# Column sums of V's weights moved from the start of a fused attention and mixer kernel into its first head-sum visit

## Chip, cores and metric

The kernel runs on one core of a Trainium2 chip, in one launch. The metric is the device time in microseconds (us), the median of several runs. A core has TensorE (PE, matmul), VectorE (DVE), ScalarE (ACT), GpSimd (POOL) and SyncE (SP), which run side by side and meet at semaphores. Each engine works through its own instructions in order. Transfers are issued by SP, ACT and POOL and carried out by 16 shared DMA engines.

## What is computed

The reference adds three terms over 2048 positions of 512 numbers: the input, a windowed attention with 32 heads of 16 numbers (window of 8 positions, every second one), and a gated mixer. Cut to what matters:

```
xn  = layernorm(x)
qkv = xn @ wqkv                       # q, k, v: 32 heads of 16
logits[s, w] = q[s] . k[s - 2w] / 4   # w = 0..7, masked where s - 2w < 0
o   = softmax(logits) weighted sum of v[s - 2w]
A   = o @ wo
z   = gelu(xn' @ w_in)                # xn' = layernorm(xn)
z1, z2 = z[:, :896], layernorm(z[:, 896:])
B   = (z1 * (w_sp @ z2 + b_sp)) @ w_out
out = x + A + B
```

For the first blocks of 128 rows V is made from the raw input, before the layernorm is known: V = rstd * (x @ wv) - rstd * mean * (column sums of wv). The column sums are the subject of the change.

## The kernel before

**Planner.** The kernel doesn't write its instructions in order. It records tasks (`T` and `dma`, line 503 on), each with an engine, what it reads and writes, an estimated duration and a priority, and `Plan.schedule` (line 123) runs a list scheduling over them. It picks, for each engine, the task that can start first; among tasks that could start within `tol` of it, the one of lowest priority number. Transfers get an assumed landing time, by bandwidth or from a table `land`, written by hand. The result is a fixed order for each engine, and semaphores where a task depends on another. An order that the planner must keep is written out by hand in lists of names (lines 1031 to 1041). The planner's times don't exist at run time; only the orders do. So a change of an estimate, a priority or a landing time moves instructions in places that the diff doesn't show.

**Tiling.** Rows are in 16 blocks of 128 (`b`), or four groups of 512 (`j`). PSUM has eight banks, given to tasks by the planner.

**Start (0 to 18 us).** SP and ACT load x, V's weights in two halves (`wv`, `ldwv0`, `ldwv1`, L532), and the second half of the mixer's weights in two (`ldwin2a`, `ldwin2b`, L538, L544). Seven matmuls on ones (`warm`, L574) run first. For blocks 0 to 2 (`NRAW`), TensorE transposes raw x (`xTx`, L593, four 128x128 matmuls), ScalarE copies the result to SBUF (`xTc`, L620), and `V0` to `V2` (L681, two tasks of two matmuls 128x512 each) multiply by wv. VectorE computes mean and variance (L613, L615), GpSimd `rstd` (L626, a power), VectorE the layernorm (`norm`, L638). From block 1 on the normalized block is transposed by a DMA (`xTd`, L632); from block 3 on V uses it directly. `z2_b` (L793) is the mixer's second half, four matmuls 128x448 for each of two halves.

**Column sums before.** `cs_0` and `cs_1` (L653) are four matmuls of a 128x128 matrix of ones with wv, 512 columns each, in two tasks: `cs_0` behind `xTx0`, `cs_1` between the two halves of `z2_0`. All 128 rows of the result are equal to the column sums. ScalarE writes them, negated, to `ncs` (`cse`, L657). ScalarE writes V's raw products, scaled by rstd, to `vraw` (L688), and VectorE makes `fix0` to `fix2` (L690): V = ncs * (mean * rstd) + vraw. Both inputs are f32 and are read through `hd`, which turns the columns from head by head to the order (number in head, head), a step of 16 elements. GpSimd's queue writes V to DRAM (`Vw`, L695, tensor `vscr`).

**Middle (18 to 97 us).** `Q` and `K` (L704), `z1` (L839) and the other V and z2 blocks fill TensorE. VectorE makes the products of q and k for 8 window positions (`prod`, L725) and adds them over 4 chunks (`padd`, L730), each instruction 128x4096. The sum over heads is TensorE's `red0` (groups 0 and 1) and `red2` (groups 2 and 3) in `logits`, L740: 16 matmuls with a 128x32 matrix `E32`, four side by side on four 32-column strips. The softmax follows (`smax`, `ssub`, L755, L757; `sexp`; `sz`, `srec`, `sattn`, L769 to L779), then a transpose (`attnT`, L781). z2's second layernorm is `z2_wave` (L812 to L825), with a power on GpSimd (`zr`, L822) and `zn` on VectorE (L825).

**Rest (97 to 234 us).** `g` (L935) is the big matmul of the mixer with w_sp, 448 matmuls 128x512; VectorE takes its results (L946, L949) and, in turn, the weighted sums of V (`pv`, L963 to L969), whose inputs `ldVs` (L958) read `vscr` from DRAM. The results are transposed by DMA (`OTd`, L972) and enter the output matmuls (`outo`, `out`, L991, L1000), four and seven for each block; VectorE adds x (`fin`, L1006), and SP stores (L1011).

Of the kernel before, what the change touches and what calls it, by code (L numbers as in the profile page):

```python
# [346 lines left out]
def build_kernel(nc, A_x, A_wqkv, A_wo, B_x, B_w_in, B_w_sp, B_b_sp, B_w_out, out, report=False, emit=True):  # L347
# [17 lines left out]
    vscr = nc.dram_tensor("vscr", (16 + S, 512), BF).ap()  # L365

# [24 lines left out]
    off["ncs"] = off["xcT"] + 512 * NRAW  # L391
    off["vraw"] = off["ncs"] + 1024
# [5 lines left out]
    for name, n in (("prime", 4), ("mx", 128), ("Zb", 256), ("Z", 128), ("maskt", 128), ("st6", NB * 6),  # L398
                    ("mv", NB * 2), ("vpe", NB), ("rstd", NB), ("s1", NB), ("s2", NB), ("m2", NB), ("msq", NB), ("mr", 4),
                    ("vpe2", NB), ("rstd2", NB), ("mhalf", 4)):  # L400
        foff[name] = fb
        fb += n
# [5 lines left out]
    with ExitStack() as es:  # L408
# [74 lines left out]
        for b in range(NRAW):  # L483
            R1(("vraw", b), "vraw", 1024, 1024 * b)
# [87 lines left out]
        for wi in range(NWARM):  # L572
# [14 lines left out]
        def pe_tr(src, keys, name):  # L587
            bk = plan.bank(name)

            def tr(t):  # L590
                last = None
                for dc in range(4):
# [3 lines left out]
            T("pe", tr, reads=keys + ["ident"], writes=[bk], est=4 * c_mm(128), name=name)  # L596
# [10 lines left out]
        def ln_block(b):  # L607
# [9 lines left out]
            if b < NRAW:  # L617
                bc = pe_tr(xin, xk, "xTx%d" % b)
                for h0, hn in ((0, 1), (1, 1)) if b < 2 else ((0, 2),):
                    T("act", (lambda h0, hn: lambda a: a.activation(A("xcT", 256 * hn, 512 * b + 256 * h0),  # L620
                                                                    P(bc, 256 * hn, 256 * h0), ACTF.Copy))(h0, hn),
# [25 lines left out]
        def colsum():  # L647
            bk = plan.bank("cs")
            for hf in range(2):
                def mm(t, hf=hf):  # L650
                    last = None
                    for dc in (2 * hf, 2 * hf + 1):
                        last = t.matmul(P(bk, 512), ones[:, 0:128], A("wv", 512, 512 * dc), start=(dc == 0),  # L653
                                        stop=(dc == 3))
                    return last
                T("pe", mm, reads=[("wv", hf)], writes=[bk], est=2 * c_mm(512) * (1 if hf else 1.6), name="cs_%d" % hf, prio=2)
            T("act", lambda a: a.activation(ncs, P(bk, 512), ACTF.Copy, scale=-1.0), reads=[bk],  # L657
              writes=["ncs"], est=c_act(512), name="cse", prio=-0.5)

        def vraw(b):  # L660
            return A("vraw", 1024, 1024 * b).bitcast(F32)

        def hd(x):
            return x.rearrange("p (h d) -> p d h", d=16)
# [6 lines left out]

        def v_block(b):
            bk = plan.bank("V%d" % b)
            sl = b % 8
            vn = A("Vn" if sl < 4 else "bbc", 512, 512 * (sl % 4))
# [11 lines left out]
            if b < NRAW:  # L687
                T("act", lambda a: a.activation(vraw(b), P(bk, 512), ACTF.Copy, scale=Fv("rstd", 1, b)),  # L688
                  reads=[bk, ("rstd", b)], writes=[("vraw", b)], est=c_act(512), name="Ve%d" % b, prio=4)
                T("dve", lambda v: v.scalar_tensor_tensor(vdh, hd(ncs), Fv("mr", 1, b), hd(vraw(b)), ALU.mult, ALU.add),  # L690
                  reads=["ncs", "mr", ("vraw", b)], writes=[("Vn", sl)], est=690, name="fix%d" % b, prio=1)
            else:
                T("act", lambda a: a.activation(vdh, PC(bk.col(), [[1, 16], [16, 32]]), ACTF.Copy),  # L693
                  reads=[bk], writes=[("Vn", sl)], est=c_act(512), name="Ve%d" % b, prio=4)
            dma("pool", lambda e: e.dma_start(vscr[16 + 128 * b: 16 + 128 * b + 128, :], vn),  # L695
                128 * 512 * 2, ("vwr", sl), reads=[("Vn", sl)], writes=[("vscr", b)], name="Vw%d" % b, prio=1)

        def qk_pair(j, c):
            bk = plan.bank("QK%d_%d" % (j, c), 2)
            for which in range(2):  # L700
                def mm(t, which=which):
# [8 lines left out]
                  est=4 * c_mm(512), name="%s%d_%d" % ("QK"[which], j, c), prio=10 + 18 * j + c)  # L710
# [6 lines left out]
        def prods(j):  # L717
            acc = (0, 2)[j % 2]
            for c in range(4):
# [7 lines left out]
                if c > 0:  # L727
# [3 lines left out]
                      reads=[("pb", 1)], writes=[("pb", acc)], est=c_tt(4096), name="padd%d_%d" % (j, c), prio=5 + j)  # L731
        def logits(j0):
# [11 lines left out]
            T("pe", mm, reads=[("pb", 0), ("pb", 2), "E32"], writes=bks, est=1050.0, name="red%d" % j0, prio=1)  # L744
# [110 lines left out]
        colsum()  # L855
# [30 lines left out]
        for j0 in range(0, NJ, 2):  # L886
# [4 lines left out]
            for j, bk in enumerate(logits(j0), j0):  # L891
                smax(j, bk)
# [138 lines left out]
        for names in (["warm%d" % wi for wi in range(NWARM)] +  # L1031
                      ["xTx0", "cs_0", "V0_0", "xTx1", "V0_1", "xTx2", "V1_0", "V1_1", "xTr0", "V2_0", "V2_1",
                       "z2_0_0", "z2_0_0b", "cs_1", "z2_0_1", "z2_1_0", "z2_1_1", "z2_2_0", "z2_2_1", "V3_0", "V3_1", "z2_3_0", "z2_3_1", "V4_0", "V4_1", "z2_4_0", "z2_4_1", "Q0_0", "Q0_1", "K0_0", "K0_1"],
                      ("rstd7", "Vw0", "Vw1", "Vw2", "Vw3"),
                      ("bnst0", "bnag0", "vpe0", "bnst1", "bnag1", "vpe1", "norm0", "bnst2", "norm1", "bnag2", "vpe2", "bnst3", "norm2",
                       "bnag3", "vpe3", "norm3", "bnst4", "bnag4", "vpe4", "mr", "norm4", "fix0", "fix1", "fix2", "bnst5"),
                      ["bnst%d" % b for b in range(5, NB)],
                      ("xTc0_0", "xTc0_1", "xTc1_0", "xTc1_1", "xTc2_0", "xTe0_0", "xTe0_2", "Ve1", "Ve0", "Ve2",
                       "z2g0", "cse", "z2g1", "z2s0"), ("ldx4", "xTd1", "xTd2", "xTd3", "xTd4", "ldq", "ldk", "ldx5", "ldx6", "ldx7", "ldwin1", "ldx8"), ("ldx15", "xTd5"),
                      *[("ldwin1", "ldx%d" % b) for b in range(9, NB)], *[("z2_4_1", "%s0_%d" % (n, c)) for n in "QK" for c in range(4)],  # L1040
                      ("V10_1", "Q3_3")):
# [4 lines left out]
        plan.schedule(tol=12.0, dma_bw=300.0, dma_lat=1600.0, overlap=35.0,  # L1046
# [53 lines left out]
```

## Time and profile before

| | us |
|---|---|
| median of 3 runs | 236.48 (236.09 to 236.64) |
| profiled execution, its own time | 235.77 |
| its span, first to last instruction | 234.5 |
| TensorE busy in the span | 230.6 (98%) |
| VectorE busy | 208.9 (89%) |
| ScalarE busy | 95.7 (41%) |
| GpSimd busy | 31.6 (13%) |

By stretches of the span, from the windows of the profile:

| us | TensorE | VectorE | ScalarE | GpSimd | DMA share |
|---|---|---|---|---|---|
| 0 to 17.5 | 16.61 | 10.29 | 12.66 | 3.83 | 0.67 |
| 17.5 to 70 | 52.24 | 48.89 | 43.19 | 19.65 | 0.78 |
| 70 to 97 | 26.89 | 26.83 | 21.46 | 8.16 | 0.47 |
| 97 to 120 | 22.89 | 21.89 | 3.60 | 0 | 0.38 |
| 120 to 194 | 73.52 | 70.62 | 14.20 | 0 | 0.98 |
| 194 to 234.5 | 38.42 | 30.40 | 0.60 | 0 | 0.59 |

A row of a timeline has the start, the duration, the engine, the line of the kernel, the operation, output and input tile, shape and count; in brackets stands the idle time ahead of it and what ended it. Matmuls overlap: one 128x512 matmul has a duration of 0.379 us in the rows, while the starts of two that follow each other are 0.216 apart. `PEld` rows are weight loads, which overlap the matmuls. `SPq` rows are issues on a queue; a DMA lands later. The granted TensorE clock is full over the span.

### The profile page before, as it was taken

Reading aid. Unit: us, or ns where it says so; the run is one execution under the profiler, and the core shown is the slowest. Engines: PE = TensorE matmul, PEld = TensorE weight load, DVE = VectorE, ACT = ScalarE, POOL = GpSimd, SP = SyncE. Lnnn points to the kernel's source line nnn. Section 1 sums busy time; section 2 is a strip of 40 time slices with the busy share of each in tenths; the row PEclk is TensorE's granted clock in tenths of the full one; section 3 lists DMA queues with packets and bytes.
Section 4 is the critical chain, followed back from the end, with each engine's and each line's share of the span. In section 5 each row is a group of like instructions: output and inputs, shape, how many; then the busy total and the mean of one; then the engine's idle time right before and its main releaser. Section 6 shows DMA issues by size and latency. Waiting matters only on the chain.

```text
span 234.5 us, 2976 instructions
## 1 busy us (share of the span) xinstructions
PE 230.6 (98%) x1105; PEld 108.6 (46%) x1126; DVE 208.9 (89%) x271; ACT 95.7 (41%) x143; POOL 31.6 (13%) x56
## 2 busy tenths in 40 slices
PE   8999999999999999999999999999999999999996
PEld 3555455555544444444444444444444444444443
DVE  4755899999999999998999898999998998999932
ACT  4898756988895898411020172011111111000000
POOL 2302981023165430000000000000000000000000
PEclk9999999999999999999999999999999999999999
DMA  6769944999305731342299999989899839953542
GB/s 221 204 190 371 247 78 104 184 239 219 79 25 198 251 113 44 67 128 96 53 358 228 261 228 276 180 183 320 250 246 324 256 66 356 310 144 98 170 116 67
DMA packets 83646, 44.26 MB, mean 189 GB/s; under 512 B 55968, under 2 KB 82992, under 8 KB 83632
## 3 DMA queue, kind: packets, MB, share of 16 engines
q1 hardware_dynamic: 82400, 41.66, 69.4%
q0 software_dynamic: 800, 2.11, 2.6%
q10 hardware_dynamic: 432, 0.30, 0.4%
q8 instruction: 9, 0.15, 0.3%
q14 instruction: 5, 0.04, 0.1%
HBM read 26.35 MB, written 4.21 MB: 130 GB/s over the span
## 4 chain that ended last, share of the span: by engine, by line
PE 98%; issue 1%; DVE 0%
PE ps L935 41%; PE ps L704 12%; PE ps L793 10%; PE ps L839 10%; PE ps L1000 10%; PE ps L681 6%; PE ps L991 6%; PE ps L574 1%; PE ps L740 1%; PE ps L593 0%; PE ps L653 0%; DVE arena L1006 0%
## 5 line engine op out<-in xcount | busy, mean ns | idle before, releaser
L935 PE MATMUL ps<-arena 128*128 128x512 bf16 x439 | 96.4, 379 | 0.6 <-issue 0.2
L935 PEld LDWEIGHTS ps<-arena 128*128 128x128 bf16 x448 | 43.7, 98 | 53.1 <-issue 0.4
L943 ACT ACTIVATE arena<-ps 128x1024 bf16<-128x1024 f32 (+1 forms) x16 | 14.7, 917 | 79.8 <-PE ps L935 79.8
L725 DVE TENSOR_TENSOR arena<-arena 128x4096 bf16<-128x4096 bf16 x16 | 36.5, 2290 | 0.1
L963 DVE TENSOR_TENSOR arena<-arena 128x4096 bf16<-128x4096 bf16 x16 | 36.5, 2284 | 0.0
L966 DVE TENSOR_TENSOR arena<-arena 128x2048 bf16<-128x2048 bf16 (+1 forms) x32 | 30.1, 950 | 0.1
L704 PE MATMUL ps<-arena 128*128 128x512 bf16 x124 | 28.6, 379 | 0.2
L730 DVE TENSOR_TENSOR arena<-arena 128x4096 bf16<-128x4096 bf16 x12 | 27.4, 2285 | 0.1
L1000 PE MATMUL ps<-arena 128*128 128x512 bf16 (+2 forms) x117 | 26.9, 366 | 0.1
L793 PE MATMUL ps<-arena 128*128 128x448 bf16 x128 | 25.7, 352 | 0.0
L839 PE MATMUL ps<-arena 128*128 128x512 bf16 x111 | 24.6, 379 | 0.1
L704 PEld LDWEIGHTS ps<-arena 128*128 128x128 bf16 x128 | 14.4, 114 | 13.2 <-ACT arena L693 0.4
L713 ACT ACTIVATE arena<-ps 128x1024 bf16<-128x1024 f32 x16 | 16.3, 1022 | 7.4 <-PE ps L704 7.4
L1006 DVE TENSOR_TENSOR arena<-ps,arena 128x512 bf16<-128x512 f32 (+2 forms) x17 | 11.2, 658 | 8.5 <-PE ps L1000 8.3
L793 PEld LDWEIGHTS ps<-arena 128*128 128x128 bf16 x128 | 12.5, 98 | 12.1
L1000 PEld LDWEIGHTS ps<-arena 128*128 128x128 bf16 x119 | 11.4, 98 | 12.8
L839 PEld LDWEIGHTS ps<-arena 128*128 128x128 bf16 x112 | 10.9, 98 | 13.2 <-ACT arena L845 0.3
L991 PE MATMUL ps<-arena 128*128 128x512 bf16 (+2 forms) x66 | 16.5, 366 | 0.1
L801 ACT ACTIVATE arena<-ps 128x896 bf16<-128x896 f32 x16 | 14.6, 914 | 3.5 <-PE ps L793 3.4
L681 PE MATMUL ps<-arena 128*128 128x512 bf16 x61 | 15.6, 379 | 0.2
L613 DVE BATCH_NORM_STATS2 fpool<-arena 128x6 f32<-128x512 bf16 x16 | 10.8, 680 | 5.5 <-DMA arena<-in_A_x_dram 5.5
L845 ACT ACTIVATE arena<-ps 128x1024 bf16<-128x1024 f32 (+1 forms) x16 | 13.9, 922 | 3.7 <-PE ps L839 3.6
(62 smaller groups left out, 171.7 us busy)
## 6 DMA issues: line engine op xcount, KB each, us to landing
arena<-vscr SPq DMA_DIRECT2D x16, 1024.0 KB, 6.5
arena<-in_A_x_dram SPq DMA_DIRECT2D x30, 128.0 KB, 3.7
vscr<-arena POOLq DMA_DIRECT2D x16, 128.0 KB, 3.1
out_dram<-arena SPq DMA_DIRECT2D x15, 128.0 KB, 1.9
arena<-in_A_wqkv_dram SPq DMA_DIRECT2D x2, 512.0 KB, 4.6
arena<-in_B_w_in_dram SPq DMA_DIRECT2D x2, 448.0 KB, 4.9
arena<-in_B_w_in_dram SPq DMA_DIRECT2D x1, 896.0 KB, 8.2
arena<-in_B_w_out_dram SPq DMA_DIRECT2D x1, 896.0 KB, 5.1
```

Source lines behind the costliest of these rows:

```text
L681: last = t.matmul(P(bk, 512), A("xcT", 128, 512 * b + 128 * dc) if b < NRAW else xTv(b, dc), A("wv", 512, 512 * dc), start=(dc == 0), stop ...
L704: last = t.matmul(P(bk, 512, 512 * which), AC(off["wqk"] + 2048 * which + 512 * dc + c, [[4, 128]]), AC(off["xnT"] + dc * S + 512 * j, [[1 ...
L713: T("act", lambda a: a.activation(AC(qo, [[ko - qo, 2], [1, 512]]), P(bk, 1024).rearrange("p (t n) -> p t n", t=2), ACTF.Copy, scale=0.5), ...
L725: T("dve", (lambda pbv, qb, kb: lambda v: v.tensor_tensor(pbv, qb, kb, ALU.mult))(pbv, qb, kb), reads=rd, writes=[("pb", s_)], est=c_tt(40 ...
L730: T("dve", (lambda av, bv: lambda v: v.tensor_tensor(av, av, bv, ALU.add))(av, bv), reads=[("pb", 1)], writes=[("pb", acc)], est=c_tt(4096 ...
L793: last = t.matmul(P(bk, 448, 512 * hf), xTv(b, dc), AC(off["w_in2"] + 896 * dc + 448 * hf, [[1, 448]]), start=(dc == 0), stop=(dc == 3))
L839: last = t.matmul(P(bk, 512, 512 * i), AC(off["w_in1"] + 896 * dc + 128 * fc, [[1, 128]]), AC(off["xnT"] + dc * S + 512 * j, [[1, 512]]), ...
L935: last = t.matmul(P(bk, 512, 512 * i), AC(off["z2"] + FH * sh + 128 * fc, [[1, 128]]), AC(off["wT%d" % r_] + sh * 512, [[1, 512]]), start= ...
L963: T("dve", lambda v: v.tensor_tensor(tv, tv, av, ALU.mult), reads=[("attn", b)], writes=[("Vs", sv)], est=c_tt(4096), name="pv%d" % b, pri ...
L966: T("dve", (lambda n: lambda v: v.tensor_tensor(A("Vs", n, 4096 * sv), A("Vs", n, 4096 * sv), A("Vs", n, 4096 * sv + n), ALU.add))(n), wri ...
L991: last = t.matmul(P(bk, cn), AC(off["OT"] + 512 * tb + 128 * cc, [[1, 128]]), AC(off["wo"] + 512 * cc + c0, [[1, cn]]), start=(cc == 0), s ...
L1000: last = t.matmul(P(bk, cn), AC(off["z1T"] + fc * S + 128 * tb, [[1, 128]]), AC(off["w_out"] + 512 * fc + c0, [[1, cn]]), start=False, sto ...
```

## The change

1. The matmuls `cs_0` and `cs_1` are gone from the start. The four column-sum matmuls now stand behind the 16 of `red0`, in the same task. Each uses 32 columns of ones and one quarter of wv's rows (128 of 512), on its own 32-column strip: the four strips hold four partial sums, each repeated on 32 rows. The bank (`csbank`) is taken for them.
2. ScalarE's `cse` writes them, negated and in the order (number in head, head), to `ncs`. Four transfers on GpSimd's queue follow, each waiting for what comes before: `csa` writes rows 0, 32, 64 and 96 (4 x 2 KB) to DRAM (`cpart`); `csb` reads them back with four columns to a partition (128 x 4 runs of 16 bytes); two GpSimd adds (`csu`, `csv`) sum the four parts; `csc` writes 512 sums to DRAM (`cscr`); `csr` reads them to all 128 partitions (256 KB).
3. `fix0` to `fix2` wait for `csr`; they are recorded behind `logits(0)`. `vraw` is now written by ScalarE in the new column order, so that VectorE reads and writes contiguously. `Vw0` to `Vw2` follow `csr` and the fixes. V of blocks 0 to 2 has its own place (`Vn0`), in the region of `z1T`, and so have `ncs` and `vraw`.
4. The first transpose `xTx0` is split into two tasks with a bank each, and an eighth warm-up matmul (128 columns) stands behind them.
5. Planner: priority of Q and K of group j from 10 + 18 j to 10 + 30 j; `tol` from 12 to 58, `dma_bw` from 300 to 285, VectorE's `overlap` from 35 to 60; landing times for the four transfers (77.0, 80.5, 83.2, 85.9 us); the lists of orders follow, with `csa` ahead of `zr2` and `csr` ahead of `zr3` on GpSimd. By these, VectorE's `fix0` stands behind the last `padd` of chunk 2 of group 2 and ahead of `zn12`, and TensorE does z2 of blocks 5 to 7 ahead of Q and K of group 1, and all V ahead of `red0`.

```diff
@@ -388,15 +390,16 @@
-    off["ncs"] = off["xcT"] + 512 * NRAW
-    off["vraw"] = off["ncs"] + 1024
+    off["Vn0"] = off["z1T"] + 1536
+    off["ncs"] = off["z1T"] + 3 * S + 1024
+    off["vraw"] = off["ncs"] + S
...
@@ -569,7 +578,7 @@
-        for wi in range(NWARM):
+        for wi in range(NWARM + 1):
...
@@ -615,10 +624,11 @@
-                bc = pe_tr(xin, xk, "xTx%d" % b)
+                bcs = [pe_tr(xin, xk, "xTx0a", (0, 1)), pe_tr(xin, xk, "xTx0b", (2, 3))] if b == 0 else [pe_tr(xin, xk, "xTx%d" % b)] * 2
...
@@ -644,24 +654,25 @@
-        def colsum():
-            bk = plan.bank("cs")
-            for hf in range(2):
-                def mm(t, hf=hf):
-                    last = None
-                    for dc in (2 * hf, 2 * hf + 1):
-                        last = t.matmul(P(bk, 512), ones[:, 0:128], A("wv", 512, 512 * dc), start=(dc == 0),
-                                        stop=(dc == 3))
-                    return last
-                T("pe", mm, reads=[("wv", hf)], writes=[bk], est=2 * c_mm(512) * (1 if hf else 1.6), name="cs_%d" % hf, prio=2)
-            T("act", lambda a: a.activation(ncs, P(bk, 512), ACTF.Copy, scale=-1.0), reads=[bk],
-              writes=["ncs"], est=c_act(512), name="cse", prio=-0.5)
+        def colsum(bk):
+            T("act", lambda a: a.activation(ncs.rearrange("p (d h) -> p d h", d=16), PC(bk.col(), [[1, 16], [16, 32]]), ACTF.Copy, scale=-1.0), reads=[bk], writes=["csp"], est=c_act(512),
+              name="cse", prio=-0.5)
+            dma("pool", lambda e: e.dma_start(cpart, A("ncs", 1024).bitcast(F32)[0:128:32, :]),
+                8192, "csa", reads=["csp"], writes=["cpart"], name="csa", prio=-5)
+            dma("pool", lambda e: e.dma_start(Fv("csq", 16).rearrange("p (q i) -> p q i", q=4),
+                                              bass.AP(tensor=cpart.tensor, offset=cpart.offset, ap=[[4, 128], [512, 4], [1, 4]])),
+                8192, "csb", reads=["cpart"], writes=["csq"], name="csb", prio=-5)
+            T("pool", lambda g: g.tensor_tensor(Fv("csq", 8), Fv("csq", 8), Fv("csq", 8, 8), ALU.add), writes=["csq"],
+              est=200, name="csu", prio=-5)
+            T("pool", lambda g: g.tensor_tensor(Fv("css", 4), Fv("csq", 4), Fv("csq", 4, 4), ALU.add), reads=["csq"],
+              writes=["css"], est=200, name="csv", prio=-5)
+            dma("pool", lambda e: e.dma_start(bass.AP(tensor=cscr.tensor, offset=cscr.offset, ap=[[4, 128], [1, 4]]), Fv("css", 4)),
+                2048, "csc", reads=["css"], writes=["cscr"], name="csc", prio=-5)
+            dma("pool", lambda e: e.dma_start(ncs, bass.AP(tensor=cscr.tensor, offset=cscr.offset, ap=[[0, 128], [1, 512]])),
+                128 * 2048, "csr", reads=["cscr"], writes=["ncs"], name="csr", prio=-5)
...
@@ -685,15 +703,15 @@
-                T("act", lambda a: a.activation(vraw(b), P(bk, 512), ACTF.Copy, scale=Fv("rstd", 1, b)),
+                T("act", lambda a: a.activation(vraw(b).rearrange("p (d h) -> p d h", d=16), PC(bk.col(), [[1, 16], [16, 32]]), ACTF.Copy,
+                                                   scale=Fv("rstd", 1, b)),
                   reads=[bk, ("rstd", b)], writes=[("vraw", b)], est=c_act(512), name="Ve%d" % b, prio=4)
-                T("dve", lambda v: v.scalar_tensor_tensor(vdh, hd(ncs), Fv("mr", 1, b), hd(vraw(b)), ALU.mult, ALU.add),
-                  reads=["ncs", "mr", ("vraw", b)], writes=[("Vn", sl)], est=690, name="fix%d" % b, prio=1)
+                fixes.append((b, vn, vk))
+                return
...
@@ -707,7 +725,7 @@
-                  est=4 * c_mm(512), name="%s%d_%d" % ("QK"[which], j, c), prio=10 + 18 * j + c)
+                  est=4 * c_mm(512), name="%s%d_%d" % ("QK"[which], j, c), prio=10 + 30 * j + c)
...
@@ -729,6 +747,14 @@
+        def fix_all():
+            for b, vn, vk in fixes:
+                def fix(b=b, vn=vn, vk=vk):
+                    T("dve", lambda v: v.scalar_tensor_tensor(vn, ncs, Fv("mr", 1, b), vraw(b), ALU.mult, ALU.add),
+                      reads=["ncs", "mr", ("vraw", b)], writes=[vk], est=690, name="fix%d" % b, prio=1)
+                fix()
+                v_write(b, vn, vk)
...
@@ -741,7 +767,18 @@
+            if j0 == 0:
+                mm0 = mm
+
+                def mm(t):
+                    mm0(t)
+                    last = None
+                    for q in range(4):
+                        last = t.matmul(ps[32 * q:32 * q + 32, csbank.col():csbank.col() + 512], ones[:, 0:32],
+                                        A("wv", 512, 512 * q), start=True, stop=True)
+                    return last
...
@@ -888,7 +925,11 @@
-            for j, bk in enumerate(logits(j0), j0):
+            lgs = logits(j0)
+            if j0 == 0:
+                colsum(csbank)
+                fix_all()
+            for j, bk in enumerate(lgs, j0):
...
@@ -1029,23 +1070,23 @@
-                      ("V10_1", "Q3_3")):
+                      ("V10_1", "Q3_3"), ("csa", "zr2"), ("csr", "zr3")):
...
-        plan.schedule(tol=12.0, dma_bw=300.0, dma_lat=1600.0, overlap=35.0,
+        plan.schedule(tol=58.0, dma_bw=285.0, dma_lat=1600.0, overlap=60.0,
```

More of the change, by code (lines that the diff above doesn't have):

```diff
@@ L483, in build_kernel @@
         for b in range(NRAW):
-            R1(("vraw", b), "vraw", 1024, 1024 * b)
+            R1(("Vn", "raw", b), "Vn0", 512, S * b)
+        R1("csp", "ncs", 1024)
+        for fc in range(FC):
+            for j in range(NJ):
+                R1(("z1T", fc, j), "z1T", 512, fc * S + 512 * j)
+        for b in range(NRAW):
+            R1(("vraw", b), "vraw", 1024, S * b)
         R1("bbc", "bbc", S)
@@ L591, in tr @@
                 last = None
-                for dc in range(4):
+                for dc in dcs:
                     last = t.matmul(P(bk, 128, 128 * dc), src[:, 128 * dc:128 * dc + 128], ident, start=True,
```

48 lines of the change are left out of this document (27 added, 21 removed).

## The prediction

> **What bounds the kernel now.** I read the chain of waits first (page, part 4), then the same chain in order of time, then the timeline where the change acts.
>
> ```profile
> PE 98%; issue 1%; DVE 0%
> ...
> 4.11 0.58 PE ps L653 x2
> ...
> 8.83 0.43 PE ps L653 x2
> ```
>
> The chain is TensorE from end to end, so a matmul taken out is worth its time only if the next one can really start earlier. The column-sum matmuls (L653) stand in it with 0.58 + 0.43 = 1.01 us. Both lie in the first 10 us, where TensorE follows the loads:
>
> ```profile
> 4.09 0.60 PE L653 MATMUL ps<-arena,const-bfloat16-1.0 128*128 128x512 bf16 x2
> 4.59 0.60 PE L681 MATMUL ps<-arena 128*128 128x512 bf16 x2
> 5.31 0.59 PE L681 MATMUL ps<-arena 128*128 128x512 bf16 x2
> ...
> 8.67 0.59 PE L653 MATMUL ps<-arena,const-bfloat16-1.0 128*128 128x512 bf16 x2
> 9.10 1.11 PE L793 MATMUL ps<-arena 128*128 128x448 bf16 x5
> ```
> ```profile
> 3.27 0.51 SPq L544 DMA_DIRECT2D arena<-in_B_w_in_dram  x1
> ...
> 6.89 5.99 SPq L632 DMA_TRANSPOSE arena<-arena  x4
> ```
>
> The second half of V's weights, issued at 1.3, takes the longer of L532's two landings, 3.9: it is there at 5.2, and V0_1 runs at 5.31. The second half of w_in2 takes 5.3 from 3.27 and is there at 8.57. The first transpose takes 2.6 from 6.89 and is there at 9.54; z2_1_0, which needs it, runs at 9.10 + 4 x 0.19 = 9.86.
>
> VectorE is the near rival (89%), so I looked at what it owes TensorE: the head sums (L740), each behind the last `padd`.
>
> ```profile
> 67.10 2.29 DVE L730 TENSOR_TENSOR arena<-arena 128x4096 bf16<-128x4096 bf16 x1
> 69.99 1.05 PE L740 MATMUL ps<-arena 128*32 128x512 bf16 x16
> ...
> 111.75 0.69 DVE L946 TENSOR_TENSOR arena<-arena 128x1024 bf16<-128x1024 bf16 x1 [1.08 <-ACT arena L943]
> 115.16 2.29 DVE L730 TENSOR_TENSOR arena<-arena 128x4096 bf16<-128x4096 bf16 x1
> 119.22 1.05 PE L740 MATMUL ps<-arena 128*32 128x512 bf16 x16
> ```
>
> red0 runs 0.6 behind its padd (69.39), red2 1.77 behind its own (117.45). VectorE has 1.08 of idle time shortly before the second.
>
> **The change, part by part.**
>
> *Start, TensorE.* cs_0 filled a wait. Without it, and with the two transposes of xTx0a evicted first, V0_0 comes some 0.2 earlier, but V0_1 still needs the weights that land at 5.2 and stays at 5.31: gain 0. The split transposes and the eighth warm-up matmul lie in that hole. cs_1 (0.43) goes too; z2_0_1 may then run at 8.67, with its weights landed at 8.57: 8.70. z2_1_0 would follow at 9.46, but its transpose is there at 9.54; V0_1 ran 0.1 behind its landing, so 9.64 instead of 9.86. Everything behind it is back to back and landed earlier (w_in1: 15.60 + 8.2 = 23.8, wanted at 24.3). Start: -0.22, between -0.30 (no delay behind the landing) and 0 (that transpose 0.2 later, with nothing left to fill the hole).
>
> *red0, TensorE.* Four matmuls 128x512 on 32 columns, as L740 has them: 16 took 119.88 - 119.22 = 0.66 to the start of the last four, so four starts lie in 0.22. They extend a visit that is paid anyway: +0.22. Were they not side by side they would cost 4 x 0.216 = 0.86 (L935's start to start), the upper bound; the lower is 0.22. I take 0.22, the same shape in the same instruction stream.
>
> *Order ahead of red0.* The order of instructions gives the changed red0 20 more V matmuls (4.31), 8 more z2 (1.51) and 24 fewer Q/K (5.18): +0.65, so it stands at 69.99 + 0.65 - 0.22 = 70.4. The rest comes behind it instead; ahead of red2 the sums are equal. VectorE's padds up to there are the same, some 0.5 later by the moved masks and `rstd` on GpSimd: 69.9. No stall; the 0.5 left is the margin.
>
> *fix0 to fix2, VectorE.* Before, they ran in a hole:
>
> ```profile
> 11.67 3.15 DVE L690 SCALAR_TENSOR_TENSOR arena<-arena,fpool 128x512 bf16<-128x512 f32 x3
> ```
> ```profile
> L757 DVE TENSOR_TENSOR arena<-ps,fpool 128x1024 bf16<-128x1024 f32 x4 | 4.9, 1220 | 0.0
> L690 DVE SCALAR_TENSOR_TENSOR arena<-arena,fpool 128x512 bf16<-128x512 f32 x3 | 3.1, 1117 | 0.0
> ```
>
> They free 3.1 us nobody used and now stand between padd2_2 and zn12, in the dense stage. Old form: 1.04 start to start, reading f32 at a 64-byte stride. The new form reads and writes contiguously. Bounds: 0.61 (half of L757's elements, less the overlap of 0.08) and 1.04 (its own row). I take 0.61, since L757 also has two f32 sources and the stride is gone: 3 x 0.61 = 1.8. The 1.08 idle ahead of L946 swallows part: red2's padd ends at 117.45 + 1.8 - 1.08 = 118.2, TensorE arrives at 119.2. Cost 0, 1.0 left. At 1.04 each it would end at 119.5: +0.4.
>
> The Trainium skill (SBUF — State Buffer, the note on cachelines under "Door 1: The DMA port swizzle") says an engine pays for each access that crosses to a new 16-byte line; L690 at 1.117 for 512 elements beside L757 at 1.220 for 1024 agrees. By it the fixes cost 0.6 each, the same sum.
>
> *The four transfers, GpSimd's queue.* cse is one ScalarE row of 0.59 (L693's strided read), done at 72.4. Then, in the queue's order: csa, zr2, csb, csu, csv, csc, csr, zr3, Vw0 to Vw2. No row has these shapes.
>
> ```profile
> vscr<-arena POOLq DMA_DIRECT2D x16, 128.0 KB, 3.1
> ...
> arena<-in_B_b_sp_dram SPq DMA_DIRECT2D x1, 512.0 KB, 4.7
> ...
> vscr<-arena POOLq DMA_DIRECT2D x1, 16.0 KB, 1.9
> ```
> ```profile
> 28.59 1.02 POOL L822 TENSOR_TENSOR fpool<-fpool 128x4 f32<-128x4 f32 x1
> ...
> 67.22 3.06 POOL L822 TENSOR_TENSOR fpool<-fpool 128x4 f32<-128x4 f32 x1 [2.27 <-DVE fpool L819]
> ```
>
> csa 2.1 (L695's median between 70 and 82 us; 1.9 to 4.0): 74.5. zr2 holds the queue to 76.0. csb, 512 runs of 16 bytes: 3.1 (1.9, up to 4.0 plus three more issues of 0.54 = 5.6): 79.1. csu and csv: two adds of 0.55 (L626's 128x1 row) plus 0.5 of waiting, since VectorE then does the short L825 rows: 1.6 (0.3, two memsets of 0.15, up to 5.2: two of 0.55 with the whole 3.06 - 1.02 = 2.04 on each): 80.7. csc 2.1 (1.9 to 4.0): 82.8. csr, 256 KB: 3.4, half way between 2.1 and 4.7: **86.2**, bounds 80.5 and 95.9.
>
> fix0 is reached when VectorE has done five padds/prods (2.2 each, start to start), two smax and two ssub (1.13 to 1.25), four L825 (0.43) and the small rows behind 69.9, 17.7 in all: 87.6. So csr is 1.4 early; with red2's 1.0, it may land until **88.6** before TensorE notices. Queued behind csr: zr3 (zn12 to zn15, wanted by g0_0_3 at 99, ready near 92) and Vw0 to Vw2 (landed near 93; ldVs1 was issued at 102.77): covered. New is ScalarE's wait: `ncs`, `vraw` and `Vn0` lie in z1T, so its L845 tasks for groups 2 and 3 wait until the fixes have read (89.5) and Vw0 to Vw2 have landed. The last of these tasks ran at 92.56, 94.29 and 96.02; two of the three writes are in by 92.5, and a held task stops TensorE only when no bank is left for the next group (two banks each, 1.73 us of matmuls). Covered, but narrowly: it falls with the same late csr.
>
> *Tail.* VectorE ends at most 0.8 later than before in the dense stage; OTd15, issued at 222.62, landed some 2.7 later (the transposes' median), at 225.3, and is wanted at 230.2. Covered.
>
> **Sum.** Against the profiled execution, 235.77 (span 234.5 and 1.27 around it): -0.22 + 0.22 + 0 = 235.8. That execution lies 0.71 below the median of the runs, 236.48, so I state **236.5**. Its own range: -0.3 to +0.4, so 236.2 to 236.9.
>
> **Rivals.**
> *A. csr lands late* (slower). VectorE runs in order, so fix0 holds all of softmax and prod3 behind it; past 88.6 each us is one us at red2, and TensorE has no idle time to win it back. For: four round trips in series in the stage where L695's landings reached 4.0, and zr1, zr2, zr3 took 3.0 for the work that took 1.02 at 28.59. With one full block of 2.04 on each add (+3.0) and 1.5 more on csb, csr comes at 90.7: +2.1, 238.6. Against: 2.4 of margin. The Trainium skill (SBUF — State Buffer, "Who interferes with whom") says a VectorE instruction with two SBUF inputs contends with a GpSimd instruction that reads SBUF; the 3.06 beside 1.02 agrees, and by that rule an add issued under a prod or padd waits it out.
> *B. The start gains all it frees* (faster). If the landings did not hold TensorE, 1.01 - 0.22 = 0.79 would be won: 235.7. For: both sums are in the chain. Against: 5.2 and 9.54 above; it needs transfers that land earlier than in this execution.
> *C. The sum matmuls run one by one*: +0.86 - 0.22 = +0.64, 237.1. Against: L740's starts.
> *D. The change's relief is nil and the fixes keep 1.04*: 236.9, inside the forecast's range.
>
> **How the numbers follow.** This kernel's measurement can tell about 0.2% (0.47 us) from no change. Forecast with D, within that: 0.46. A: 0.34. C or another stall (red0's 0.5 margin used up): 0.05. B: 0.15. So faster 0.15, same 0.46, slower 0.39. The range runs from 235.8 (most of B left outside) to 239.4, A with csr at 91.5; about 0.07 lies above.
>
> **What would show it.** V0_1 near 5.31 and z2_1_0 near 9.6: the start. red0 with 20 matmuls near 70.4, some 0.22 longer: the sum. The fixes at 0.69 each: the stride. csr's landing against fix0's start: if VectorE idles ahead of fix0 on a DMA, A is at work, and red2 shows the same delay less 1.0. I am wrong if red2 waits for VectorE, or if z2_1_0 starts before 9.5.

## The result, and the profile after

| | before | after |
|---|---|---|
| median of 22 runs, us | 236.2 (235.71 to 236.83) | 237.41 (236.08 to 238.53) |
| profiled execution, us | 235.77 | 237.73 |
| its span, us | 234.5 | 236.5 |

The ratio is 1.0048, with a 95% interval of 1.0035 to 1.0062: about half a per cent slower. The two profiled executions differ by 1.96, the medians by 1.21: the first profile lies 0.43 below its median, the second 0.32 above its own.

The page of the changed kernel, part 4, the chain that ended last. Before, it was TensorE at 98%.

```profile
PE 74%; DVE 14%; DMA 8%; issue 2%; POOL 1%; ACT 1%; ACTq 0%
```

Transfers and VectorE have entered it. The same chain in order of time (start, duration, what), from the first transfer of the column sums to the second head sum; short pieces called issue, between one transfer and the next, are left out:

```profile
73.18 3.04 DMA cpart<-arena
76.51 5.02 DMA fpool<-cpart
81.89 2.38 POOL fpool L667
84.55 1.70 DMA cscr<-fpool
86.54 3.86 DMA arena<-cscr
90.42 2.08 DVE arena L753 x3
...
121.16 1.05 PE ps L766 x16
```

csa, csb, the adds, csc and csr stand one behind the other, then the fixes (L753), VectorE's products and sums, and red2 (L766). The timeline of the changed kernel shows what each end of this did to its engine:

```profile
71.58 0.39 PE L777 MATMUL ps<-arena,const-bfloat16-1.0 128*32 128x512 bf16 x4
...
81.89 2.37 POOL L667 TENSOR_TENSOR fpool<-fpool 128x4 f32<-128x4 f32 x1
81.91 2.29 DVE L743 TENSOR_TENSOR arena<-arena 128x4096 bf16<-128x4096 bf16 x1
...
90.42 2.08 DVE L753 SCALAR_TENSOR_TENSOR arena<-arena,fpool 128x512 bf16<-128x512 f32 x3 [2.90 <-DMA arena<-cscr]
...
121.16 1.05 PE L766 MATMUL ps<-arena 128*32 128x512 bf16 x16 [1.42 <-DVE arena L748]
```

VectorE idles 2.90 us ahead of the fixes, for csr. 31 us later TensorE idles 1.42 ahead of red2, for VectorE: an engine that is busy from there on passes its delay to the next meeting point. By the starts of TensorE's matmuls, the 1.96 us divide into +0.07 at the start, +0.22 in red0's visit, a wait of 0.16 ahead of the matmul at 93.67 (z1, whose ScalarE evictions stand behind the fixes), and +1.49 at red2: 1.94 in all.

### The profile page after: what moved, and what is told of

Read it like the earlier page. It is cut to its first block, busy times and chain, and to the rows that moved or that the text cites. A ratio compares the mean times of both kernels' runs of the same rounds, so it can differ in the third digit from the quotient of the medians.

```text
span 236.5 us, 3005 instructions
## 1 busy us (share of the span) xinstructions
PE 232.0 (98%) x1127; PEld 108.3 (46%) x1127; DVE 207.2 (88%) x271; ACT 95.9 (41%) x143; POOL 33.4 (14%) x62
## 4 chain that ended last, share of the span: by engine, by line
PE 74%; DVE 14%; DMA 8%; issue 2%; POOL 1%; ACT 1%; ACTq 0%
PE ps L976 31%; PE ps L1041 10%; PE ps L830 10%; PE ps L722 9%; PE ps L1032 6%; PE ps L699 5%; DVE arena L748 4%; DVE arena L743 4%; PE ps L876 3%; DMA fpool<-cpart 2%; DMA arena<-cscr 2%; DMA cpart<-arena 1%; DMA arena<-arena 1%; DMA arena<-in_A_x_dram 1%; POOL fpool L667 1%
```

## The experiments

Eleven kernels in three sets, each beside runs of the kernel before on the same chip (medians 236.07, 236.22 and 236.31 in the first, second and third set).

| kernel | set | runs | median, us | ratio (95% interval) |
|---|---|---|---|---|
| free_fix | 1 | 12 | 236.17 | 1.0000 (0.9987 to 1.0012) |
| wide_sums | 1 | 4 | 238.17 | 1.0084 (1.0066 to 1.0102) |
| few_runs | 1 | 6 | 237.65 | 1.0071 (1.0043 to 1.0098) |
| quiet_loads | 1 | 11 | 235.93 | 0.9993 (0.9981 to 1.0005) |
| one_more_trip | 2 | 6 | 240.95 | 1.0169 (1.0130 to 1.0208) |
| wide_pinned | 2 | 12 | 236.60 | 1.0012 (0.9999 to 1.0025) |
| no_sums | 2 | 12 | 237.36 | 1.0026 (1.0001 to 1.0050) |
| planner_only | 2 | 12 | 236.85 | 1.0033 (1.0020 to 1.0045) |
| no_sums_warm | 3 | 12 | 236.03 | 0.9990 (0.9978 to 1.0002) |
| quiet_no_warm | 3 | 12 | 236.10 | 0.9991 (0.9978 to 1.0004) |
| early_trip | 3 | 12 | 236.30 | 0.9997 (0.9981 to 1.0013) |

The ratios are of each kernel to the kernel before in its own set. The runs of no_sums fall into two groups 1.0 us apart, so its median stands for neither.

**Is it the wait for csr? free_fix** takes the wait away: csr writes to a place of its own, and the fixes read what cse wrote. All else stays.

```diff
-            dma("pool", lambda e: e.dma_start(ncs, bass.AP(tensor=cscr.tensor, offset=cscr.offset, ap=[[0, 128], [1, 512]])),
+            dma("pool", lambda e: e.dma_start(ncx, bass.AP(tensor=cscr.tensor, offset=cscr.offset, ap=[[0, 128], [1, 448]])),
...
-                      reads=["ncs", "mr", ("vraw", b)], writes=[vk], est=690, name="fix%d" % b, prio=1)
+                      reads=["csp", "mr", ("vraw", b)], writes=[vk], est=690, name="fix%d" % b, prio=1)
```

> The changed kernel with its instructions in the same order on every queue and all four transfers still made, but the last one writes 448 of its 512 columns to a place of its own, and fix0 to fix2 read what cse wrote. It leaves out the true column sums for blocks 0 to 2. Theory (the fixes wait for the sums, and red2 waits for VectorE): the 2.90 us of VectorE idle ahead of the fixes goes, padd3_3 ends near 118.2 instead of 121.1, TensorE reaches red2 near 119.6 and does not wait, so the 1.58 us gap goes and the 0.16 us one behind it: 235.7 us (235.4 to 236.2). Rival (the fixes' load in the dense stage, or the new order of the stage, costs the time): red2 still waits for VectorE and the time stays at 237.0 or more.

Timeline of free_fix:

```profile
87.19 2.07 DVE L756 SCALAR_TENSOR_TENSOR arena<-arena,fpool 128x512 bf16<-128x512 f32 x3
...
119.25 1.05 PE L769 MATMUL ps<-arena 128*32 128x512 bf16 x16
```

No bracket stands behind either row: the fixes follow the row ahead of them at once, and red2 doesn't wait. The time is that of the kernel before. By the trace every engine runs its instructions in the changed kernel's order, and the trip was late here too (csr issued at 85.03, 4.6 to land, so 89.6). The new order of the dense stage and the fixes' 2.07 us in it therefore cost nothing that can be measured; the wait costs it all.

**What makes csr late? few_runs** reads the four partial sums in longer runs, **quiet_loads** keeps SP's loads out of the way.

```diff
-                                              bass.AP(tensor=cpart.tensor, offset=cpart.offset, ap=[[4, 128], [512, 4], [1, 4]])),
+                                              bass.AP(tensor=cpart.tensor, offset=cpart.offset, ap=[[32, 16], [512, 4], [1, 32]])),
```
```diff
+        for n1 in ["ldbbc"] + ["ldwo%d" % c for c in range(4)] + ["ldxr%d" % c for c in range(4)]:
+            byname[n1].deps.add(byname["csr"])
```

> The changed kernel with csb, the adds and csc on 16 partitions: 64 runs of 128 bytes instead of 512 of 16. If csb's 5.02 us come from its many short runs, it falls toward csa's 3.04, csr lands near 88.4 instead of 90.4, VectorE's idle ahead of the fixes falls from 2.90 to 0.9, padd3_3 ends near 119.1 ahead of TensorE at 119.6, and the time is 235.8 us (235.4 to 236.4). If the length comes from the transfers of SyncE that run beside it, csb keeps 4.5 to 5.0, and the time stays at 237.2 to 237.5.

> The changed kernel with ldbbc, ldwo0 to ldwo3 and ldxr0 to ldxr3 held until csr has landed, so that nothing of SyncE's runs beside the trip. If these loads stretch it, csb falls from 5.02 to 3 and csr from 3.86 to 3, csr lands near 87.6 and the time is 235.8 us (235.4 to 236.4). If they do not, csr lands at 90 or later and the time is 237.2 to 237.5, or more where a held load is itself late.

DMA issues of the changed kernel between 72 and 91 us: size, and us from issue to landing.

```profile
arena<-cscr POOLq DMA_DIRECT2D x1, 256.0 KB, 3.9
...
cpart<-arena POOLq DMA_DIRECT2D x1, 8.0 KB, 3.0
fpool<-cpart POOLq DMA_DIRECT2D x1, 8.0 KB, 5.0
cscr<-fpool POOLq DMA_DIRECT2D x1, 2.0 KB, 1.7
```

The same of few_runs (72 to 96 us):

```profile
arena<-cscr POOLq DMA_DIRECT2D x1, 256.0 KB, 4.7
cpart<-arena POOLq DMA_DIRECT2D x1, 8.0 KB, 3.8
fpool<-cpart POOLq DMA_DIRECT2D x1, 8.0 KB, 4.1
cscr<-fpool POOLq DMA_DIRECT2D x1, 2.0 KB, 2.8
```

And of quiet_loads (72 to 90 us):

```profile
arena<-cscr POOLq DMA_DIRECT2D x1, 256.0 KB, 3.8
...
cpart<-arena POOLq DMA_DIRECT2D x1, 8.0 KB, 1.7
fpool<-cpart POOLq DMA_DIRECT2D x1, 8.0 KB, 2.4
cscr<-fpool POOLq DMA_DIRECT2D x1, 2.0 KB, 1.8
```

In few_runs csb is 0.9 shorter, and the three others took 0.7 to 1.1 longer in that execution; csr landed at 90.46 and nothing was won. About 3 was expected for csb if its short runs were the cause. The 4.1 measured is no gain that can be told from scatter: with the short runs as they were and the same loads beside it, csb took 4.0 in free_fix and 4.4 in one_more_trip. So the short runs are not the cause.

With SP's queue silent csa takes 1.7 instead of 3.0 and csb 2.4 instead of 5.0, and csr lands at 85.46 instead of 90.40. Only SP's transfers have changed their places in the trace of quiet_loads; every other queue keeps its order. Of the 4.94, the two transfers give 3.7 from issue to what follows them; 0.9 comes from the adds, of which VectorE held up one in either kernel, for longer in the changed one, and 0.36 from csa's earlier issue. The packets of the two traces show how the loads act on csb, which is 16 packets of 512 bytes. The first starts 1.53 us after the issue in both (at 78.04 and 76.55). The last starts 3.86 after it in the changed kernel and 1.81 in quiet_loads. In the changed kernel SP's packets start in the same time: those of 4 KB (ldbbc) until 78.37, those of 1 KB (ldxr and ldwo) from 78.51 to 82.17. In quiet_loads SP has none there.

csr itself took as long (3.8 beside 3.9). That doesn't make it free of neighbours: it took 4.7 in few_runs, and 6.6 in early_trip, where the DMA engines were busy throughout (DMA share 1.19 from 45.8 to 52.4). The timeline of quiet_loads at red2:

```profile
119.15 1.05 PE L766 MATMUL ps<-arena 128*32 128x512 bf16 x16
```

Red2 follows TensorE's work without a wait. The held loads (0.5 MB of ldbbc, four of 128 KB for ldxr, and ldwo) were not wanted earlier, so holding them cost nothing. Which of them does most of the harm was not tried. The amount of traffic alone does not say it: the kernel before moved 219 GB/s between 70 and 82 us, and its nine writes of V in that time (128 KB each) took 2.1 us at the median; the changed kernel moved 148 GB/s while csb ran.

**Does the end follow csr one for one? one_more_trip** makes csr later by one transfer.

```diff
+            dma("pool", lambda e: e.dma_start(cscr2.rearrange("(a b) -> a b", a=16), cscr.rearrange("(a b) -> a b", a=16)), 2048, "csd", reads=["cscr"], writes=["cscr2"], name="csd", prio=-5)
...
-                128 * 2048, "csr", reads=["cscr"], writes=["ncs"], name="csr", prio=-5)
+                128 * 2048, "csr", reads=["cscr2"], writes=["ncs"], name="csr", prio=-5)
```

> The changed kernel with one transfer more in the chain: the 2 KB of cscr are copied to a second DRAM buffer before csr reads them from there; nothing else moves. Theory (the end follows csr's landing one for one): the added trip takes 2 to 3 us (csc 1.70, csa 3.04), csr lands at 92.4 to 93.4, red2 waits 2 to 3 us longer, and the time is 239.4 to 240.4 us. Rival (fixes' load or order): under 238.2, since nothing on an engine was added.

The chain of one_more_trip, again without the pieces called issue, and a row of its timeline:

```profile
85.14 4.62 DMA cscr<-cscr
90.05 3.38 DMA arena<-cscr
93.46 2.08 DVE arena L755 x3
```
```profile
96.71 1.89 PE L878 MATMUL ps<-arena 128*128 128x512 bf16 x4 [2.83 <-ACT arena L884]
```

csr lands 3.0 later than in the changed kernel (93.44), and the span is 3.1 longer (239.6). The added transfer took 4.6 where 2 to 3 were expected, and the median, 240.95, is above the range given. That the two differences agree does not show the end following csr one for one, since the place of the charge has moved: TensorE waits at 96.71 for ScalarE's z1 evictions (L884), which wait for the fixes to read `ncs` and `vraw`, and red2 no longer waits for VectorE. The cover that the prediction called narrow is gone here. The windows of one_more_trip add a second charge (columns: stretch; its length; busy us and instructions of TensorE, its weight loads, VectorE, ScalarE and GpSimd; the granted clock; DMA share; GB/s):

```profile
96.70:98.00 1.30, 1.29 (x4) 0.47 (x5) 1.30 (x4) 1.30 (x3) 0.00 (x0) 0.50 0.45 180
98.00:100.00 2.00, 2.00 (x7) 0.76 (x6) 2.00 (x2) 1.46 (x3) 0.00 (x0) 0.59 0.00 0
100.00:101.80 1.80, 1.80 (x10) 0.78 (x8) 1.80 (x2) 1.03 (x2) 0.00 (x0) 1.00 0.05 9
```

After an idle time of 2.83 us (3.21 from one start to the next) TensorE got half its clock for some 3 us: its matmuls come 0.43 apart until 99.65, which costs 1.4. So the 3.1 are made of a wait of 3.0 in the place of 1.65, of 1.4 for the clock, and of 0.2 by which TensorE was later ahead of it. The other runs agree: the two with a mean granted clock of 1.0 took 238.63 and 239.10 us, the three with 0.993 took 240.84 to 241.49, the one with 0.986 took 242.23. A long stall can be paid twice; by these clocks it was in four of the six runs. In the changed kernel, where TensorE idled 1.42, the granted clock behind it is 1.00 (121 to 125 us), and all its runs have a mean of 1.0.

**What do the sums cost when they need no trip? wide_sums and wide_pinned** make them whole in red0's visit.

```diff
-                        last = t.matmul(ps[32 * q:32 * q + 32, csbank.col():csbank.col() + 512], ones[:, 0:32],
-                                        A("wv", 512, 512 * q), start=True, stop=True)
+                        last = t.matmul(P(csbank, 512), ones[:, 0:128],
+                                        A("wv", 512, 512 * q), start=(q == 0), stop=(q == 3))
...
-            dma("pool", lambda e: e.dma_start(cpart, A("ncs", 1024).bitcast(F32)[0:128:32, :]),
-                8192, "csa", reads=["csp"], writes=["cpart"], name="csa", prio=-5)
...
```

> The changed kernel with the column sums made whole in red0's visit: four matmuls with 128 columns of ones, accumulated, and cse writes ncs at once; the four transfers and the two adds are gone. Theory (only the trip is late): no VectorE idle ahead of the fixes, red2 does not wait; the four matmuls cost 0.86 instead of 0.22, so 235.7 + 0.65 = 236.4 us (236.0 to 236.8), no slower than before by more than 0.3. Rival (fixes or order cost it): 237.4 or more.

> wide_sums once more (four matmuls with 128 columns of ones, accumulated, no transfers), now with every engine's instructions held in the changed kernel's order, where wide_sums had been planned anew and TensorE waited 1.3 us for a late transpose at its end. Theory (only the trip is late; order and fixes cost nothing): no wait at red2 and none at the end; the visit costs 0.65 more than four matmuls of 32 columns, so free_fix's 236.17 + 0.65 = 236.8 us (236.4 to 237.1). Rival (the new order itself costs): 237.4 or more.

wide_sums missed its range, 238.17 against at most 236.8. Without the transfers the planner had made another order, and its timeline shows the price at the end:

```profile
232.46 0.82 PE L1019 MATMUL ps<-arena 128*128 128x384 bf16 x4 [1.15 <-DMA arena<-arena]
```

TensorE waits for the last transpose of O by 1.3 us, from the starts of its matmuls. With the order held, in wide_pinned, that wait is gone, as is red2's; the four matmuls cost what was expected:

```profile
70.57 1.05 PE L753 MATMUL ps<-arena 128*32 128x512 bf16 x16
71.55 1.04 PE L764 MATMUL ps<-arena,const-bfloat16-1.0 128*128 128x512 bf16 x4
72.43 1.89 PE L709 MATMUL ps<-arena 128*128 128x512 bf16 x8
```

72.43 - 70.57 = 1.86 for the visit, against 71.91 - 70.71 = 1.20 in the changed kernel: 0.66 more (0.65 expected). The time, 236.60, lies in the range given and below the changed kernel's 237.41 of the earlier runs. The chain of transfers saved 0.66 us of TensorE and cost 1.65.

**Does the planner's new order cost something? planner_only** is the kernel before with the change's settings.

```diff
-                  est=4 * c_mm(512), name="%s%d_%d" % ("QK"[which], j, c), prio=10 + 18 * j + c)
+                  est=4 * c_mm(512), name="%s%d_%d" % ("QK"[which], j, c), prio=10 + 30 * j + c)
...
-        plan.schedule(tol=12.0, dma_bw=300.0, dma_lat=1600.0, overlap=35.0,
+        plan.schedule(tol=58.0, dma_bw=285.0, dma_lat=1600.0, overlap=60.0,
```

> The kernel before with only the planner's settings of the change (due times of Q and K 30 instead of 18 apart, tolerance 58, rate 285, overlap 60); the sums stay at the start. If the moved order of the dense stage costs nothing by itself, 235.8 to 236.4 us; if it were the cause, some 237.3.

```profile
4.08 1.04 PE L653 MATMUL ps<-arena,const-bfloat16-1.0 128*128 128x512 bf16 x2
...
69.73 1.05 PE L740 MATMUL ps<-arena 128*32 128x512 bf16 x16 [0.33 <-DVE arena L730]
```

The timeline shows red0 waiting for its padd, 0.40 by the starts of the matmuls. In this execution the start also came 0.42 later, since the matmuls were 0.4 apart until 5.3 us, cs_0 (L653) among them, where the kernel before has 0.23 from 4.1 on. Together that is its 0.8 of span over the kernel before. How many of the twelve runs had the slower start is not known. The median, 236.85, lies between the two values expected. It doesn't explain the change, whose red0 didn't wait and whose order, in free_fix, ran as fast as before.

**What were the sums worth at the start? no_sums** is the kernel before without them; **no_sums_warm** adds one warm-up matmul behind the first transposes; **quiet_no_warm** takes that matmul from quiet_loads.

```diff
...
-                T("pe", mm, reads=[("wv", hf)], writes=[bk], est=2 * c_mm(512) * (1 if hf else 1.6), name="cs_%d" % hf, prio=2)
-            T("act", lambda a: a.activation(ncs, P(bk, 512), ACTF.Copy, scale=-1.0), reads=[bk],
-              writes=["ncs"], est=c_act(512), name="cse", prio=-0.5)
+            T("pool", lambda g: g.memset(ncs, 0.0), writes=["ncs"], est=600, name="ncs0", prio=-9)
...
```

no_sums_warm has this beside it:

```diff
-        for wi in range(NWARM):
+        for wi in range(NWARM + 1):
...
```

> The kernel before without its column sums: cs_0, cs_1 and cse are gone, GpSimd writes zeros to ncs; it leaves out the correction of blocks 0 to 2 by the sums. Forecast of the prediction: cs_0 fills a wait for wv1 and is worth nothing, cs_1's 0.43 is worth 0.2 to 0.4 as the first transpose then limits, so 235.7 to 235.9 us. Rival (both sums stand on the path): 0.8 to 1.0 less than before, 235.1 to 235.3.

> no_sums with one more warm-up matmul (128x128) behind the first transposes, as the changed kernel has it. In no_sums 8 of 12 runs were at 237.3 to 238.0 and 4 at 235.6 to 236.3; in the profiled slow one TensorE idled 0.82 us ahead of V0_0, and its matmuls of 512 columns came every 0.43 us until 9.5 us, where they come every 0.216 in the kernel before. Theory (what keeps TensorE busy ahead of V0_0 keeps its matmuls fast): with the filler all runs lie at 235.5 to 236.2. Rival (something else of the start, such as a late load): the runs stay split, with 237.3 and more among them.

> quiet_loads (235.93 us) without the warm-up matmul that the change added behind the first two transposes. Theory (the filler keeps the matmuls fast): some or most runs come to 237.5 to 238.2, with matmuls of 512 columns every 0.43 us until about 9.5 us. Rival (a filler in a hole is worth nothing, as the prediction had it): all runs at 235.6 to 236.4.

no_sums became slower: work was taken away, and 7 of its 12 runs lie at 237.3 to 238.0, 5 at 235.6 to 236.3 (8 and 4 in the expectation of no_sums_warm is a wrong count). The timeline of its profiled execution (237.83):

```profile
4.85 1.01 PE L671 MATMUL ps<-arena 128*128 128x512 bf16 x2 [0.57 <-ACT arena L620]
...
7.36 1.91 PE L671 MATMUL ps<-arena 128*128 128x512 bf16 x4
```

The same matmuls in no_sums_warm:

```profile
4.01 0.31 PE L574 MATMUL ps<-const-bfloat16-1.0 128*128 128x128 bf16 x1
4.69 0.61 PE L671 MATMUL ps<-arena 128*128 128x512 bf16 x2 [0.37 <-ACT arena L620]
...
7.10 1.03 PE L671 MATMUL ps<-arena 128*128 128x512 bf16 x4
```

Four matmuls take 1.91 in the one and 1.03 in the other: in no_sums they start every 0.43 us until about 9.5, in no_sums_warm every 0.216 from 4.7 on. With the filler all 12 runs lie at 235.7 to 236.5, the split is gone, and the top is 0.3 above the range expected. So work in cs_0's place had a use that a hole doesn't show: with nothing there (0.82 us by the starts, 0.57 in the bracket) the matmuls stay at half speed for 5 us more in that execution. That it helps by keeping TensorE busy ahead of V0_0 was the theory. The Trainium skill ("TensorE: Matmul & The Clock Gate", "What's actually happening") says the array runs at half clock until a window of about 3.4 us was busy, and that this window runs free, so that the moment varies from run to run; the split runs of no_sums agree. quiet_no_warm went against this theory: with a hole of 0.61 by the starts and no filler all of its 12 runs lie at 235.73 to 236.65. Nor is a full place enough: planner_only, with cs_0 in it, was slow until 5.3 in its profiled execution, and early_trip, with the filler, until 7.0. So the filler was needed in no_sums and not in quiet_no_warm; what exactly decides, the length of the hole or where it falls in time, stays open.

The sums' own worth at the start is 0.28 us by the medians of no_sums_warm (236.03 against 236.31), but its interval reaches past 1 (0.9978 to 1.0002), and in the profiled execution Q0 begins only 0.08 earlier than in the kernel before (17.56 against 17.64). So the 0.2 to 0.4 expected for no_sums is not excluded and not shown; its rival of 0.8 to 1.0 is excluded by the interval.

**Could the trip be made early? early_trip** puts the change's four matmuls at the start and the four transfers on GpSimd's idle time from 33 us on.

```diff
+        for hf in range(2):
+            def csmm(t, hf=hf):
+                last = None
+                for q in (2 * hf, 2 * hf + 1):
+                    last = t.matmul(ps[32 * q:32 * q + 32, csbank.col():csbank.col() + 512], ones[:, 0:32],
+                                    A("wv", 512, 512 * q), start=True, stop=True)
+                return last
+            T("pe", csmm, reads=[("wv", hf)], writes=[csbank], est=250.0, name="cs_%d" % hf, prio=2)
+        colsum(csbank)
...
```

> The changed kernel with the four column-sum matmuls at the start, on 32 columns as in the change: two behind the added warm-up matmul, two behind V0_1; cse follows behind z2g1, and the four transfers and two adds stand on GpSimd behind rstd15, in its idle time from 33 to 44 us. All else keeps its order, SyncE's loads too. Theory: csr lands near 46, 41 us ahead of the fixes, red2 does not wait, and red0's visit is 0.22 shorter than in quiet_loads (235.93), of which the start takes back 0.06 to 0.2: 235.7 to 236.0 us. Rival (the start pays for each matmul that stands in it): 236.2 or more.

Timeline of early_trip:

```profile
4.88 1.03 PE L699 MATMUL ps<-arena 128*128 128x512 bf16 x2
...
88.31 2.07 DVE L753 SCALAR_TENSOR_TENSOR arena<-arena,fpool 128x512 bf16<-128x512 f32 x3
```

csr lands at 52.4 (46 was expected), and the fixes don't wait. But the matmuls at the start hold V0_0 until 4.88, and in this execution the matmuls run at half speed until 7.0 (two take 1.03), so that Q0 begins 1.1 later than in the changed kernel. This execution, at 237.02, is the slowest of the twelve, so it doesn't stand for the median. 236.30 is above the theory's range and in the rival's, but the kernel before is 0.24 slower in this set than in the first, from which the range was worked out; with that the theory's range would end at 236.24, and the two can't be told apart. What is shown is that early_trip equals the kernel before (ratio 0.9997). No kernel here beat the kernel before by more than can be measured; quiet_loads, quiet_no_warm and early_trip bring the change back to its time.

## Why the prediction was partly right

The range, 235.8 to 239.4, held the 237.41. It held it because it was drawn to take in rival A: the likeliest case, no change at 236.5 (0.46), fell, and rival A, csr late (0.34), is what happened.

**The sum matmuls** were right: side by side, +0.216 in red0's visit for the 0.22 forecast.

**The fixes** were right where it mattered: 0.75 each and 2.07 for three, 0.67 start to start where 0.61 was taken, far from the 1.04 of the strided form. They cost nothing in free_fix.

**The margin** was right: VectorE was ready for the fixes at 90.42 - 2.90 = 87.52, where 87.6 was forecast. csr could land until 88.6, it landed at 90.40, 1.8 too late, and TensorE paid 0.16 + 1.49 = 1.65. "I am wrong if red2 waits for VectorE" came true as it was put. The rule of one us at red2 for each us past 88.6 held for this landing and not for the next: at 93.44, in one_more_trip, the wait came at z1 and the clock was charged on top.

**The step that failed** is csr's landing, 86.2 forecast against 90.40. Terms of that sum, forecast and measured: cse done 72.4 and 72.9; csb's issue 76.0 and 76.51; csb 3.1 and 5.02; the adds 1.6 and 2.73 (81.53 to 84.26); csc 2.1 and 1.99; csr 3.4 and 4.15, the last two with 0.29 from what they wait for to the issue, which the prediction left out. 86.2 + 0.5 + 1.9 + 1.1 - 0.1 + 0.75 is 90.35 (the first 0.5 holds for cse and csb's issue: it was csa, 3.04 for the 2.1 forecast, that held csb back until 76.51, and not zr2, done at 75.40). The largest term is csb. The bounds given were wide enough (80.5 to 95.9), but the value was taken from rows of the kernel before, where other transfers run beside them: which of SP's transfers would be in flight during the trip was not asked. In the changed kernel SP issued ldwo0 at 72.02, ldbbc at 74.15, ldwo1 at 76.05 and the ldxr at 78.17, ahead of the trip and in the middle of it; before, the first ldxr stood at 72.05, but ldbbc only at 84.96. quiet_loads, which takes these neighbours away, has csr at 85.46, close to the forecast of 86.2.

**The adds**: csv started 0.02 us ahead of a VectorE product and lasted 2.37, as long as that (2.29), where csu took 0.20. It met that product because csb was late: the adds were forecast for 79.1 to 80.7, where VectorE did the short rows. Rival A had allowed one full block of 2.04 on each add; one of the two got it. The Trainium skill (SBUF — State Buffer, "Who interferes with whom") names the port pair that VectorE and GpSimd share and calls it an exclusive lock; the trace agrees in that the add ends only when VectorE's instruction does, 0.06 us behind it (84.26 and 84.20), and so do csu in quiet_loads (1.36 long) and both adds in early_trip (1.48 and 2.23), by 0.06 to 0.07.

**The start**: -0.22 forecast, +0.07 measured in the changed kernel. The mechanism was right and its inputs moved: z2_0_1 ran at 8.93 instead of 8.70, behind a later landing of w_in2's second half, and the first transpose, issued at 6.91 where the kernel before has 6.89, landed at 9.87 instead of 9.54, so that z2_1_0 waited for it until 9.92. In quiet_loads, with the same start, it landed at 9.5, and red0 ran at 70.35, where 70.4 was forecast. Over four executions with this start (changed kernel, free_fix, few_runs, quiet_loads) it landed between 9.5 and 10.18. What moves it wasn't tried.

**The fillers**: the prediction set the split transposes and the eighth warm-up matmul down as work in a hole, worth nothing. That such work can decide whether TensorE is fast from 4.7 or from 9.5 us, as in no_sums and no_sums_warm, is missing in it. It did no harm to the number, since the change replaced one filler by another.

**The price of rival A**, 238.6 for csr at 90.7, was too high against the medians. 235.77 + 1.8 gives 237.6 for a landing at 90.4, and the profiled execution has 237.73; the 0.71 added for the median of three runs was 0.43 over 22 runs, and the median execution is 0.3 faster than the profiled one. Its sum has a slip as well: a block of 2.04 on each add raises them from the 1.6 taken to 5.2, which is 3.6 and not 3.0, so that by its own terms csr would have come at 91.3.

## What to carry to other kernels

A chain of small dependent transfers is priced with the transfers that other queues will have in flight then, and that is read from the new order of their issues; here the neighbours took 3.7 us of a trip of 17, and holding loads that nobody wanted yet gave them back. A difference that comes out as expected is taken apart into its waits before it is called one for one. The engine that waits for the chain should not be the one that feeds the bound engine, or its margin should be as large as the trip's scatter. Before a filler at the start is taken out, look at the spacing of the matmuls behind it, not only at whether its hole is free.

## What the runs showed of the hardware that was not expected

- TensorE at half speed after a pause: behind 2.83 us idle in the middle of one_more_trip the granted clock was 0.50 to 0.59 for some 3 us. The Trainium skill ("TensorE: Matmul & The Clock Gate", "What's actually happening") puts the pause that brings this at a window of about 3.4 us; here less was enough.
- At the start of no_sums, behind a pause of 0.82 us, the matmuls came 0.43 us apart until 9.5 us in the profiled run, while PEclk shows 1.00 there: in this stage only the spacing of the matmuls tells it.
- The same 8 KB took between 2.4 us (quiet_loads) and 5.0 (changed kernel) to be read into SBUF, and a copy of 2 KB from DRAM to DRAM 4.6 (one_more_trip).
